# A fused attention and FFN kernel: second batch's attention values in FFN banks, two-bank first FFN blocks, packed sums, more filler matmuls

## The chip, the cores and the metric

One core of one Trainium2 chip. The metric is device time in microseconds (us) of one execution. Where several executions were taken, the median is given. Ratios are the mean time of one kernel's runs over that of the other's of the same rounds, so they are not quite the ratio of the medians that are quoted.

Engines: PE is TensorE, DVE is VectorE, ACT is ScalarE, POOL is GpSimd, SP is SyncE. `L358` in a profile line is line 358 of the kernel; the lines used here have the same numbers in both kernels.

## The reference

```python
# q, k, v: (8, 8, 1024, 64)   E, F: (64, 1024)   w_in: (512, 2048)   w_out: (2048, 512)
k_proj = einsum('ks,bhsd->bhkd', E, k)
v_proj = einsum('ks,bhsd->bhkd', F, v)
scores = q @ k_proj.T / sqrt(64)                  # per batch and head: 1024 x 64
attn   = softmax(scores)
x      = (attn @ v_proj), heads put side by side  # (8192, 512)
out    = (max(x @ w_in, 0) ** 2) @ w_out          # (8192, 512)
```

## The kernel before

Each batch has 1024 tokens, taken as two chunks of 512. For a chunk, FFN does 16 first-layer blocks (4 matmuls of 128x512 each) and then the second layer, in groups of 4 matmuls. Each block or group is a step; a batch has 64 steps. The attention of the next batch is woven in: `at(n, stage)` runs a stage behind step n. Batch 0 has no batch ahead of it, so its own second half runs during its own FFN, and batch 1's attention comes late in the same FFN.

```python
aps = tile_pool(name="aps", bufs=2, space=PSUM)   # attention: 2 tiles of 2 banks
fps = tile_pool(name="fps", bufs=4, space=PSUM)   # FFN and the rest: 4 banks, taken in turn
out_pool = tile_pool(name="outp", bufs=4)         # output rows on their way to memory

def sums(self, pr):                    # packed: two head pairs in one PSUM tile
    ps = att_psum()
    for j in range(2):
        for o, par, a, r in VALUE_QUADS:
            c = 32 * (2 * a + j)
            nc.tensor.matmul(ps[c:c + 32, par], lhsT=ones[r, 0:32], rhs=self.e[pr + j][r, par], ...)
    rs = [soft_pool.tile(...) for _ in range(2)]
    nc.scalar.activation(rs[1][:], ps[:], AF.Ln)                    # L294
    nc.scalar.activation(rs[0][:], rs[1][:], AF.Exp, scale=-1.0)    # L295
    nc.scalar.activation(rs[1][:], rs[1][:], AF.Exp, scale=-1.0)    # L296
    for j in range(2):
        for a in range(2):             # each half-filled tile is completed by copies, L300
            nc.vector.tensor_copy(rs[j][lack:lack + 32], rs[j][have:have + 32])

def chunk_sums(self, c, g):            # plain: one head group, no copies
    ps = att_psum()
    self.sums_mm(ps, self.e[g])
    self.rs[g] = self.inverse(ps)      # Ln and one Exp

def values(self, pr, spare=False):     # spare: in two FFN banks, else in an attention tile
    ...                                # matmuls L312, then xT = values * rs on VectorE, L316

def store(self, c, tb, ps):
    o = out_pool.tile([P, DM], F32)
    nc.scalar.copy(o, ps)              # L371
    nc.sync.dma_start(out_rows[...], o)  # L373
```

Filler matmuls on zeros, `warm(n)`, keep TensorE active in the startup, before the first FFN. (`...` marks cuts.)

The softmax here doesn't subtract the row's maximum and nothing guards it: scores larger than these inputs give would overflow.

Of the kernel before, what the change touches and what calls it, by code (L numbers as in the profile page):

```python
# [18 lines left out]
def kernel(  # L19
# [49 lines left out]
    def bank(shape=(P, 512), dtype=F32):  # L69
        return fps.tile(list(shape), dtype, tag="bank", name="ps_bank")  # L70
# [18 lines left out]
    K0, Q0, V0 = (qkv_pool.tile([P, H, NI, D], BF16, name=n) for n in ("K_sb", "Q_sb", "V_sb"))  # L89
# [42 lines left out]
    def projection(name, e_bf):  # L132
        ps = bank([P, NI, KP], BF16)
        view = e_bf[:].rearrange("k (p i) -> k i p", i=NI)
        for i in range(NI):
            nc.tensor.transpose(ps[:, i, :], view[:, i, :], ident[0:KP, 0:KP])
        t = const_pool.tile([P, NI, KP], BF16, name=name)
        nc.vector.tensor_copy(t[:], ps[:])
        return t

    def warm(n):

        ps = bank()
        for _ in range(n):
            nc.tensor.matmul(ps[:], lhsT=zeros[:, 0:P], rhs=zeros[:], start=True, stop=True)
# [5 lines left out]
    class Attention:  # L151
# [29 lines left out]
        def project(self):  # L181
            ps = bank()
            for i in range(NI):
                f, l = i == 0, i == NI - 1
                nc.tensor.matmul(ps[LO, :], lhsT=ET[:, i, :], rhs=self.K[:, :, i, :], start=f, stop=l)  # L185
                nc.tensor.matmul(ps[HI, :], lhsT=FT[:, i, :], rhs=self.V[:, :, i, :], start=f, stop=l)
            for g in range(2):
# [11 lines left out]
        def project_v(self, g):  # L199

            ps = bank()
            for i in range(NI):
                for o in (LO, HI):
                    nc.tensor.matmul(
                        ps[o, 0:C // 2], lhsT=FT[:, i, :], rhs=V0[:, half[g], i, :],
                        start=(i == 0), stop=(i == NI - 1),
# [138 lines left out]
    class Ffn:  # L345
# [29 lines left out]
        def steps(self):  # L375
            for c in range(2):
                self.hsq[c] = hsq_pool.tile([P, NFB, TCH], BF16, name="hsq")
                first = self.cold and c == 0
                fb0 = 0
                if first:  # L380

                    banks = [bank() for _ in range(4)]
                    for g, fbs in ((0, (0, 1)), (0, (2, 3)), (1, (0, 1)), (1, (2, 3))):
                        for fb in fbs:
                            for cb in (2 * g, 2 * g + 1):
                                self.first_mm(c, fb, cb, banks[fb])
                            if g == 1:
                                self.square(c, fb, banks[fb])
                        yield
                    fb0 = 4  # L390
                for fb in range(fb0, NFB):
                    ps = bank()
                    for cb in range(NCB):
                        self.first_mm(c, fb, cb, ps)
                    self.square(c, fb, ps)
                    yield
                if first:

                    for t0 in range(0, 4, 2):
                        banks = [bank() for _ in range(2)]  # L400
                        for j in range(WP):
                            for t in range(2):
                                for fb in range(j * fn, (j + 1) * fn):
                                    self.second_mm(c, t0 + t, fb, banks[t])
                                if j == WP - 1:
                                    self.store(c, t0 + t, banks[t])
                                yield
                else:
                    last = self.b == B - 1 and c == 1
                    for tb in range(4):  # L410
                        if last and tb == 3:

                            for m in (slice(0, DM // 2), slice(DM // 2, DM)):
                                ps = bank()
                                for fb in range(NFB):
                                    self.second_mm(c, tb, fb, ps, m)
                                self.store(c, tb, ps, m)
                            break
                        ps = bank()
                        for j in range(WP):  # L420
                            for fb in range(j * fn, (j + 1) * fn):
                                self.second_mm(c, tb, fb, ps)
                            if j == WP - 1:
                                self.store(c, tb, ps)
                            yield

    with tc.manual_schedule(engines={PE}):
        e_bf = soft_pool.tile([KP, S], BF16, tag="expT", name="e_bf")
        nc.vector.tensor_copy(e_bf[:], e_f32[:])
        warm(8)  # L430
        ET = projection("ET", e_bf)
        warm(3)
        att = Attention(0)
        att.project_k(0)
        att.transpose_q_chunk(0, Q0, 0)
        att.transpose_k((0,))
        warm(1)
        att.chunk_scores(0, 0)
        FT = projection("FT", f_bf)
        att.project_k(1)  # L440
        att.chunk_sums(0, 0)
        att.transpose_q_chunk(0, Q0, 1)
        att.transpose_k((1,))
        warm(2)
        att.chunk_scores(0, 1)
        warm(4)
        att.project_v(0)
        att.chunk_sums(0, 1)
        warm(1)
        att.chunk_values(0, 0)  # L450
        warm(1)
        att.project_v(1)

        coming = None
        for b in range(B):
            plan = {}

            def at(step, fn, *args, **kwargs):
                plan.setdefault(step, []).append(lambda: fn(*args, **kwargs))

            if b == 0:
                at(1, att.chunk_values, 0, 1)
                at(20, att.transpose_q_chunk, 1, Q0, 0)
                at(20, att.transpose_q_chunk, 1, Q0, 1)
                at(22, att.chunk_scores, 1, 0)
                at(22, att.chunk_scores, 1, 1)
                at(25, att.chunk_sums, 1, 0)
                at(25, att.chunk_sums, 1, 1)
                at(29, att.chunk_values, 1, 0)
                at(29, att.chunk_values, 1, 1)  # L470
                nxt = Attention(1)
                nxt.load()
            if b + 1 < B:
                if b + 2 < B:
                    coming = Attention(b + 2)
                    coming.load()
                if b == 0:
                    at(36, nxt.project)
                    at(37, nxt.transpose_q, 0)
                    at(37, nxt.transpose_q, 1)  # L480
                    at(39, nxt.transpose_k)
                    at(41, nxt.scores, 0)
                    at(41, nxt.scores, 1)
                    at(43, nxt.transpose_q, 2)
                    at(43, nxt.transpose_q, 3)
                    at(45, nxt.sums, 0)
                    at(45, nxt.values, 0)
                    at(51, nxt.values, 1, True)
                    at(51, nxt.scores, 2)
                    at(51, nxt.scores, 3)  # L490
                    at(55, nxt.sums, 2)
                    at(55, nxt.values, 2)
                    at(55, nxt.values, 3, True)
                else:
                    at(14, nxt.scores, 0)
                    at(14, nxt.scores, 1)
                    at(18, nxt.sums, 0)
                    at(18, nxt.values, 0, True)
                    at(18, nxt.scores, 2)
                    at(27, nxt.values, 1)  # L500
                    at(27, nxt.scores, 3)
                    at(49, nxt.sums, 2)
                    at(49, nxt.values, 2)
                    at(49, nxt.values, 3, True)
                if b + 2 < B:
                    if b == 0:
                        at(61, coming.project)
                        at(63, coming.transpose_q_dma)
                        at(64, coming.transpose_k)
                    else:  # L510
                        at(27, coming.project)
                        at(30, coming.transpose_q_dma)
                        at(29, coming.transpose_k_dma)
            for step, _ in enumerate(Ffn(att, b == 0).steps(), 1):
                for stage in plan.pop(step, []):
                    stage()
            assert not plan, plan
            att, nxt = nxt, coming
# [30 lines left out]
```

## Time and profile before

| | before |
|---|---|
| time | 513.74 us, median of 3 (513.23 to 514.64); 513.52 of 6 |
| span in the profile | 511.5 us |
| TensorE busy | 98% |
| start of batch 1's FFN | 91.94 us |
| from there to the end | 419.6 us |

The page of the profile, kernel before: the span, one engine line of its first part (busy us, share of the span, instructions) and the granted clock and DMA rows in 40 slices.

```profile
span 511.5 us, 6926 instructions
...
PE 502.2 (98%) x2756; PEld 223.6 (44%) x2756; DVE 213.6 (42%) x433; ACT 273.7 (54%) x412; POOL 32.1 (6%) x44
...
PEclk9999999999999999999999999999999999999999
DMA  9999999899996199104931060100102011010102
```

TensorE has hardly any idle time to win, and what there is lies in the first slices, where the DMA row is full as well. One slice is 12.8 us, so the full part reaches past 60 us.

The waits of TensorE over the whole span, kernel before (who waited for whom: us in total, times, longest):

```profile
PE ps_bank L194 <- DMA K_sb<-in_k_dram: 1.2, 2, 0.6
...
PE ps_bank L241 <- DMA Q_sb<-in_q_dram: 0.8, 1, 0.8
PE ps_att L256 <- DVE xT L316: 0.8, 1, 0.8
PE ps_bank L231 <- DMA Q_sb<-in_q_dram: 0.7, 2, 0.4
...
PE ps_bank L358 <- DVE xT L341: 0.2, 1, 0.2
```

The timeline of TensorE, kernel before (start, length, engine, line, operation, in the brackets the idle time before it and what ended it). The length is modelled for pipelined matmuls; the start of the next group is the safer end of a group.

```profile
20.88 1.04 PE L358 MATMUL ps_bank<-xT,w_in_114 128*128 128x512 bf16 x4
...
22.19 1.04 PE L358 MATMUL ps_bank<-xT,w_in_116 128*128 128x512 bf16 x4
23.12 0.38 PE L358 MATMUL ps_bank<-xT,w_in_114 128*128 128x512 bf16 x1
23.72 0.81 PE L358 MATMUL ps_bank<-xT,w_in_114 128*128 128x512 bf16 x3 [0.22 <-DVE xT L341]
...
39.64 1.07 PE L231 MATMUL ps_bank<-ident,Q_sb 128*128 128x128 bf16 x16 [0.44 <-DMA Q_sb<-in_q_dram]
...
58.30 1.04 PE L358 MATMUL ps_bank<-xT,w_in_118 128*128 128x512 bf16 x4
60.16 1.07 PE L241 MATMUL ps_bank<-ident,Q_sb 128*128 128x128 bf16 x16 [0.82 <-DMA Q_sb<-in_q_dram]
...
76.05 0.39 PE L256 MATMUL ps_att<-qT,kT 64*64 64x512 bf16 x4
77.19 0.41 PE L256 MATMUL ps_att<-qT,kT 64*64 64x512 bf16 x4 [0.76 <-DVE xT L316]
```

A 128x512 matmul starts 0.216 us after the one before it in an undisturbed stretch (16 in 3.45 us). The four at 58.30 should be done at 59.16, but the next group starts at 60.16: a hole of 1.00 us. In the same way there is a hole of 0.60 us before 39.64. The four small scores matmuls at 76.05 take about 0.22 us by their starts (the like-sized group of L312 just before them took 0.24), so the hole before 77.19 is about 0.92 us. After 92 us the table of waits has nothing. So the change has about 2.5 us to win after 25 us, and something before that.

The windows view, kernel before (stretch and its length; busy us and instructions of PE, PEld, DVE, ACT, POOL; then the granted clock, the DMA share and GB/s):

```profile
8.50:11.90 3.40, 2.29 (x30) 1.49 (x31) 1.59 (x4) 1.39 (x2) 1.49 (x2) 1.00 1.28 202
11.90:15.30 3.40, 3.40 (x22) 2.17 (x23) 0.75 (x2) 0.95 (x1) 1.48 (x2) 0.50 1.28 206
```

For 3.4 us the clock was at half after a stretch in which TensorE was busy for 2.3 of 3.4 us. The length agrees with the Trainium skill ("TensorE: Matmul & The Clock Gate", Part 1), which gives a free-running window of 3413 ns whose activity sets the clock to half or full.

### The profile page before, as it was taken

The page shows a single profiled execution, that of the slowest core. Times are in us where ns is not written, and L with a number is a line of the kernel's source. Part 1 is how long each engine was busy: PE and PEld are TensorE (multiplying, and loading weights), DVE is VectorE, ACT ScalarE, POOL GpSimd, SP SyncE. Part 2 cuts the span into 40 slices and gives each one's busy share as a digit, 9 for nine tenths or more (in the row PEclk, how much of TensorE's full clock was granted, in tenths as well). Part 3 has the DMA queues.
Part 4 walks back from the last instruction along what each step waited for, and adds up shares of the span by engine and source line. Part 5 has one row for each costly group of instructions (what it writes and reads, how often), then busy time and mean ns, then how long its engine had stood idle before and what let it go on. Part 6 is the DMA issues. An engine that isn't in the chain of part 4 may idle for free.

```text
span 511.5 us, 6926 instructions
## 1 busy us (share of the span) xinstructions
PE 502.2 (98%) x2756; PEld 223.6 (44%) x2756; DVE 213.6 (42%) x433; ACT 273.7 (54%) x412; POOL 32.1 (6%) x44
## 2 busy tenths in 40 slices
PE   7999999999999999999999999999999999999997
PEld 3444444444444444444444444444444444444444
DVE  2441666544444445345352354434443443522130
ACT  2565475673637556375654837366472755544351
POOL 7320100121000020001000000000000000000000
PEclk9999999999999999999999999999999999999999
DMA  9999999899996199104931060100102011010102
GB/s 161 204 205 222 227 207 201 129 217 205 195 214 124 43 183 210 71 0 91 201 88 45 1 161 16 60 24 32 63 1 81 2 41 42 25 59 21 62 1 82
DMA packets 67840, 53.92 MB, mean 105 GB/s; under 512 B 29152, under 2 KB 59616, under 8 KB 67808
## 3 DMA queue, kind: packets, MB, share of 16 engines
q0 software_dynamic: 30880, 29.49, 36.4%
q1 hardware_dynamic: 36928, 23.99, 17.8%
q8 instruction: 21, 0.34, 0.3%
q14 instruction: 11, 0.09, 0.1%
HBM read 59.24 MB, written 16.78 MB: 149 GB/s over the span
## 4 chain that ended last, share of the span: by engine, by line
PE 87%; DMA 11%; issue 1%; DVE 0%; POOL 0%; ACT 0%; POOLq 0%; ACTq 0%
PE ps_bank L364 40%; PE ps_bank L358 40%; DMA Q_sb<-in_q_dram 6%; DMA w_in_122<-in_moe_w_in_dram 3%; PE ps_bank L185 2%; DMA K_sb<-in_k_dram 2%; PE ps_att L256 1%; PE ps_att L290 1%; PE ps_att L312 1%; PE ps_bank L312 1%; PE ps_bank L241 0%; DVE rs L300 0%; ACT rs L296 0%; POOL K_sb L76 0%; DVE xT L316 0%
## 5 line engine op out<-in xcount | busy, mean ns | idle before, releaser
L355 DVE TENSOR_TENSOR hsq<-h_relu 128x512 bf16<-128x512 bf16 x256 | 108.7, 425 | 192.5 <-ACT h_relu L354 191.8
L354 ACT ACTIVATE h_relu<-ps_bank 128x512 bf16<-128x512 f32 x256 | 151.8, 599 | 69.5 <-PE ps_bank L358 69.4
L364 PEld LDWEIGHTS <-hsq 128*128 128x128 bf16 x1040 | 99.7, 98 | 122.9 <-issue 9.3
L371 ACT COPY o_sb<-ps_bank 128x512 f32<-128x512 f32 (+1 forms) x65 | 37.5, 579 | 111.1 <-PE ps_bank L364 105.0
L364 PE MATMUL ps_bank<-w_out_128,hsq 128*128 128x512 bf16 (+1 forms) x260 | 65.8, 376 | 0.0
L364 PE MATMUL ps_bank<-w_out_124,hsq 128*128 128x512 bf16 (+1 forms) x260 | 65.7, 376 | 0.0
L364 PE MATMUL ps_bank<-w_out_131,hsq 128*128 128x512 bf16 (+1 forms) x260 | 65.6, 376 | 0.0
L364 PE MATMUL ps_bank<-w_out_126,hsq 128*128 128x512 bf16 (+1 forms) x260 | 65.6, 376 | 0.0
L358 PE MATMUL ps_bank<-xT,w_in_122 128*128 128x512 bf16 x256 | 59.1, 379 | 0.0
L358 PE MATMUL ps_bank<-xT,w_in_118 128*128 128x512 bf16 x256 | 58.2, 379 | 0.0
L358 PE MATMUL ps_bank<-xT,w_in_120 128*128 128x512 bf16 x256 | 58.2, 379 | 0.0
L300 DVE COPY rs<-rs 32x1024 f32<-32x1024 f32 x56 | 38.6, 690 | 42.3 <-ACT rs L295 41.5
L270 ACT ACTIVATE expT<-ps_att 128x1024 bf16<-128x1024 f32 x32 | 31.8, 1023 | 25.3 <-PE ps_att L256 25.2
L358 PEld LDWEIGHTS <-w_in_122 128*128 128x128 bf16 x256 | 24.5, 98 | 31.2 <-issue 2.7
L358 PEld LDWEIGHTS <-w_in_120 128*128 128x128 bf16 x256 | 24.9, 98 | 30.1 <-issue 0.4
L358 PEld LDWEIGHTS <-w_in_118 128*128 128x128 bf16 x256 | 24.9, 98 | 29.9 <-issue 0.4
L358 PE MATMUL ps_bank<-xT,w_in_114 128*128 128x512 bf16 x128 | 30.6, 379 | 0.2 <-DVE xT L341 0.2
L358 PE MATMUL ps_bank<-xT,w_in_116 128*128 128x512 bf16 x128 | 30.4, 379 | 0.0
L316 DVE TENSOR_TENSOR xT<-ps_att,rs 128x512 bf16<-128x512 f32 x28 | 18.1, 686 | 9.2 <-PE ps_att L312 8.9
L294 ACT ACTIVATE rs<-ps_att 128x1024 f32<-128x1024 f32 x14 | 14.3, 1023 | 12.7 <-PE ps_att L290 12.7
L358 PEld LDWEIGHTS <-w_in_114 128*128 128x128 bf16 x128 | 12.4, 98 | 15.3 <-issue 0.9
L358 PEld LDWEIGHTS <-w_in_116 128*128 128x128 bf16 x128 | 12.4, 98 | 15.1 <-issue 0.2
(71 smaller groups left out, 236.6 us busy)
## 6 DMA issues: line engine op xcount, KB each, us to landing
out_dram<-o_sb SPq DMA_DIRECT2D x63, 256.0 KB, 2.0
K_sb<-in_k_dram POOLq DMA_DIRECT2D x7, 1024.0 KB, 22.2
V_sb<-in_v_dram POOLq DMA_DIRECT2D x7, 1024.0 KB, 26.7
Q_sb<-in_q_dram POOLq DMA_DIRECT2D x7, 1024.0 KB, 14.8
K_sb<-in_k_dram POOLq DMA_DIRECT2D x2, 512.0 KB, 7.0
V_sb<-in_v_dram POOLq DMA_DIRECT2D x2, 512.0 KB, 11.1
Q_sb<-in_q_dram POOLq DMA_DIRECT2D x2, 256.0 KB, 7.5
w_in_118<-in_moe_w_in_dram POOLq DMA_DIRECT2D x1, 512.0 KB, 14.9
```

The costliest lines, as they stand in the source:

```text
L185: nc.tensor.matmul(ps[LO, :], lhsT=ET[:, i, :], rhs=self.K[:, :, i, :], start=f, stop=l)
L256: nc.tensor.matmul(ps[o, par], lhsT=self.kT[r, h % 4, h // 4, :], rhs=self.qT[r, h, n, :], start=True, stop=True)
L270: nc.scalar.activation(e[:], ps[:], AF.Exp, scale=SCALE)
L294: nc.scalar.activation(rs[1][:], ps[:], AF.Ln)
L300: nc.vector.tensor_copy(rs[j][lack:lack + 32], rs[j][have:have + 32])
L312: nc.tensor.matmul(ps_x[par][o], lhsT=self.vp[r, 2 * pr + a, :], rhs=e[r, par], start=True, stop=True)
L316: nc.vector.tensor_tensor(out=self.xT[:, pr, :, par], in0=ps_x[par].rearrange("p (c t) -> p c t", c=2), in1=rs[:, par].rearrange("p (c t) ...
L354: nc.scalar.activation(r[:], ps[:], AF.Relu)
L355: nc.vector.tensor_tensor(out=self.hsq[c][:, fb, :], in0=r[:], in1=r[:], op=ALU.mult)
L358: nc.tensor.matmul(ps[:], lhsT=w_in_blk(cb, fb), rhs=self.xT[:, cb, c].rearrange("p a t -> p (a t)"), start=(cb == 0), stop=(cb == NCB - 1),)
L364: nc.tensor.matmul(ps[:, m], lhsT=self.hsq[c][:, fb, tb * P:(tb + 1) * P], rhs=w_out_blk(fb)[:, m], start=(fb == 0), stop=(fb == NFB - 1),)
L371: nc.scalar.copy(o[:, m], ps[:, m])
```

## The change

The intent has three parts: fillers to keep the clock full and first FFN blocks that hold two banks, not four; Q transposes later, so that they do not wait for their load; batch 1's first values in FFN's banks, so that the attention tile is free for the scores. The second half's sums become packed. Cut to its core:

```diff
-                    banks = [bank() for _ in range(4)]
-                    for g, fbs in ((0, (0, 1)), (0, (2, 3)), (1, (0, 1)), (1, (2, 3))):
-                        for fb in fbs:
+                    banks = [bank() for _ in range(2)]
+                    for g in range(2):
+                        for fb in range(2):
 ...
-                    fb0 = 4
+                    fb0 = 2
 ... fillers: 3 -> 4, +1, 1 -> 3, +3, 4 -> 2, one moved: five more in all ...
-                at(20, att.transpose_q_chunk, 1, Q0, 0)      # and the second; scores 22 -> 23
+                at(21, att.transpose_q_chunk, 1, Q0, 0)
-                at(25, att.chunk_sums, 1, 0)
-                at(25, att.chunk_sums, 1, 1)
+                at(26, att.sums, 0)
 ...
-                    at(37, nxt.transpose_q, 0)               # and 1
+                    at(39, nxt.transpose_q, 0)
-                    at(43, nxt.transpose_q, 2)               # and 3
+                    at(44, nxt.transpose_q, 2)
                     at(45, nxt.sums, 0)
-                    at(45, nxt.values, 0)
-                    at(51, nxt.values, 1, True)
-                    at(51, nxt.scores, 2)
+                    at(48, nxt.values, 0, True)
+                    at(48, nxt.scores, 2)
+                    at(51, nxt.values, 1)
                     at(51, nxt.scores, 3)
```

More of the change, by code (lines that the diff above doesn't have):

```diff
@@ L431 @@
         ET = projection("ET", e_bf)
-        warm(3)
+        warm(4)
         att = Attention(0)
         att.project_k(0)
+        warm(1)
         att.transpose_q_chunk(0, Q0, 0)
         att.transpose_k((0,))
-        warm(1)
+        warm(3)
         att.chunk_scores(0, 0)
         FT = projection("FT", f_bf)
+        warm(3)
         att.project_k(1)
@@ L445 @@
         att.chunk_scores(0, 1)
-        warm(4)
+        warm(2)
         att.project_v(0)
+        warm(1)
         att.chunk_sums(0, 1)
-        warm(1)
         att.chunk_values(0, 0)
@@ L462 @@
                 at(1, att.chunk_values, 0, 1)
-                at(20, att.transpose_q_chunk, 1, Q0, 0)
-                at(20, att.transpose_q_chunk, 1, Q0, 1)
-                at(22, att.chunk_scores, 1, 0)
-                at(22, att.chunk_scores, 1, 1)
-                at(25, att.chunk_sums, 1, 0)
-                at(25, att.chunk_sums, 1, 1)
+                at(21, att.transpose_q_chunk, 1, Q0, 0)
+                at(21, att.transpose_q_chunk, 1, Q0, 1)
+                at(23, att.chunk_scores, 1, 0)
+                at(23, att.chunk_scores, 1, 1)
+                at(26, att.sums, 0)
                 at(29, att.chunk_values, 1, 0)
@@ L478 @@
                     at(36, nxt.project)
-                    at(37, nxt.transpose_q, 0)
-                    at(37, nxt.transpose_q, 1)
+                    at(39, nxt.transpose_q, 0)
+                    at(39, nxt.transpose_q, 1)
                     at(39, nxt.transpose_k)
@@ L483 @@
                     at(41, nxt.scores, 1)
-                    at(43, nxt.transpose_q, 2)
-                    at(43, nxt.transpose_q, 3)
+                    at(44, nxt.transpose_q, 2)
+                    at(44, nxt.transpose_q, 3)
                     at(45, nxt.sums, 0)
-                    at(45, nxt.values, 0)
-                    at(51, nxt.values, 1, True)
-                    at(51, nxt.scores, 2)
+                    at(48, nxt.values, 0, True)
+                    at(48, nxt.scores, 2)
+                    at(51, nxt.values, 1)
                     at(51, nxt.scores, 3)
```

## The prediction

> **What bounds the kernel now.** TensorE. The page gives PE 98% of a 511.5 us span, and later batches repeat every 60.4 us in the chain of waits with no PE wait in the waits table. So only the first 92 us can change. Comparing starts of successive PE groups in the timeline with 0.216 us per 128x512 matmul, about 10 us there is not useful matmul time, most of it before 25 us. After 25 us only three holes matter: 0.60 us before the second-half Q transposes (39.64), 1.00 us before batch 1's Q transposes (60.16, "DMA Q_sb"), and 0.92 us before one scores group (77.19, "DVE xT"). The chain of waits follows DMA up to 60.16: queues move about 205 GB/s without a break, so loads land at fixed times whatever PE does.
>
> **Startup fillers.** Windows show the clock at 0.50 from about 11.9 to 15.3 us; there eight K-projection matmuls take 1.81 us instead of 0.87. That is one 3.4 us window, as the Trainium skill says ("TensorE: Matmul & The Clock Gate", Part 1: idle window halves the clock). Net five more fillers cost 1.1 us of matmul time but sit mostly in holes (0.39 us at 10.2, 0.59 at 11.85); I give 70% that the clock then stays full. PE gets about 1.3 us ahead before FFN, but V halves land near 15.9 and 18.4 and w_in near 19.7 and 22.
>
> **First FFN blocks over two banks.** This removes useful work: before, w_in_116 matmuls filled 22.19 to 23.12 while VectorE evicted xT. Now PE waits for that eviction (about 1.2 us). Estimated net lead after these blocks: 0.4 us.
>
> **Sums of the second half.** Moving the Q transposes one step later hides the 0.6 us hole; lead about 0.8 us. One packed sums group (0.34 us for 8) replaces two plain ones (0.56), and ScalarE does three 1.0 us passes, not four. But VectorE gets four new 0.69 us rs copies behind the last passes. Estimate: sums at 45.7, Ln and two Exp to 49.3, copies to 51.0, four xT products (0.62 each) to 53.5, while PE wants the last xT block at 52.5. A new wait of about 1 us at the start of the second FFN chunk eats the lead: about 0 left.
>
> **Batch 1.** Q transposes two steps (1.73 us) later: the 1.00 us hole goes. Values in FFN banks with scores a step group earlier should free the attention bank, so the 0.92 us wait for xT goes. But the first second-layer matmul now needs the bank of the relu which queues behind a 1.06 us Exp: a new wait of about 0.4 us. Net 0.3 to 0.5.
>
> **Sum.** 0.0 + 1.0 + 0.3 gives about 1.3 us saved, 0.25%; nothing later changes. Prediction 512.5 us, 80% range 511.2 to 513.7. Faster by over 2%: 0.01; within 2%: 0.98; slower by over 2%: 0.01.
>
> **What would show it.** Right: clock 1.0 through 11.9 to 15.3; a PE wait for xT (L341) near 21 to 22.5 and again near 52; four rs copies (L300) near 48 to 51; no PE wait for Q_sb at 60; no PE wait of 0.8 us for xT (L316), instead a short one for a relu near 74; batch period still 60.4 us. Wrong: clock still halved; no xT wait near 52 (then up to 2.3 us saved); Q_sb landing later than 60.1 us.
>
> **What would make it wrong.** The clock window may fall differently in each run; the rs copies may take longer while another engine shares the memory port; the scores two steps after the transposes may wait for qT or kT.

## The result

| | before | after |
|---|---|---|
| median of 6 | 513.52 us (513.23 to 514.64) | 512.41 us (512.14 to 512.76) |
| ratio | | 0.9976, 95% interval 0.9963 to 0.9988 |
| span in the profile | 511.5 us | 510.6 us |
| start of batch 1's FFN | 91.94 us | 91.03 us |
| from there to the end | 419.6 us | 419.6 us |

The time fell by 1.1 us, and the whole saving in the profiles (0.9 us) is there when batch 1's FFN starts. All outputs are right.

The page of the profile, kernel after:

```profile
span 510.6 us, 6940 instructions
...
PE 501.5 (98%) x2761; PEld 223.0 (44%) x2761; DVE 216.9 (42%) x437; ACT 272.8 (53%) x411; POOL 32.3 (6%) x44
```

The windows view, kernel after, for the stretch whose clock was at half before:

```profile
11.90:15.30 3.40, 2.88 (x34) 1.78 (x34) 1.64 (x4) 1.60 (x2) 1.48 (x2) 1.00 1.29 205
```

The waits of TensorE, kernel after:

```profile
PE ps_bank L358 <- DVE xT L341: 1.8, 5, 0.9
...
PE ps_bank L358 <- DMA w_in_114<-in_moe_w_in_dram: 0.6, 1, 0.6
PE ps_bank L194 <- DMA K_sb<-in_k_dram: 0.4, 1, 0.4
PE ps_bank L204 <- DMA V_sb<-in_v_dram: 0.3, 1, 0.3
```

The three waits named above are gone. In their place stands one for xT, five times, and waits for loads in the startup. The timeline of PE, DVE and ACT, kernel after:

```profile
20.36 1.04 PE L358 MATMUL ps_bank<-xT,w_in_114 128*128 128x512 bf16 x4 [0.63 <-DMA w_in_114<-in_moe_w_in_dram]
...
22.60 0.38 PE L358 MATMUL ps_bank<-xT,w_in_114 128*128 128x512 bf16 x1 [0.87 <-DVE xT L341]
...
49.11 2.80 DVE L300 COPY rs<-rs 32x1024 f32<-32x1024 f32 x4 [6.93 <-ACT rs L295]
51.94 2.48 DVE L341 TENSOR_TENSOR xT<-ps_att,rs 128x512 bf16<-128x512 f32 x4
52.69 0.38 PE L358 MATMUL ps_bank<-xT,w_in_114 128*128 128x512 bf16 x1
53.28 0.38 PE L358 MATMUL ps_bank<-xT,w_in_114 128*128 128x512 bf16 x1 [0.22 <-DVE xT L341]
53.88 0.38 PE L358 MATMUL ps_bank<-xT,w_in_114 128*128 128x512 bf16 x1 [0.22 <-DVE xT L341]
54.48 1.24 PE L358 MATMUL ps_bank<-xT,w_in_114 128*128 128x512 bf16 x5 [0.22 <-DVE xT L341]
...
61.83 1.06 PE L241 MATMUL ps_bank<-ident,Q_sb 128*128 128x128 bf16 x16
...
70.37 1.02 ACT L294 ACTIVATE rs<-ps_att 128x1024 f32<-128x1024 f32 x1
71.28 0.60 ACT L354 ACTIVATE h_relu<-ps_bank 128x512 bf16<-128x512 f32 x1
...
72.70 0.61 ACT L354 ACTIVATE h_relu<-ps_bank 128x512 bf16<-128x512 f32 x1
73.36 1.04 PE L364 MATMUL ps_bank<-w_out_124,hsq 128*128 128x512 bf16 x4
...
76.30 0.39 PE L256 MATMUL ps_att<-qT,kT 64*64 64x512 bf16 x4
76.62 1.04 PE L364 MATMUL ps_bank<-w_out_131,hsq 128*128 128x512 bf16 x4
```

The brackets show only 0.22 us of idle before each matmul at 53.28, 53.88 and 54.48, because a matmul's modelled length is 0.38. By the starts, each came 0.60 us after the one before it, not 0.216: three times 0.38, or 1.14 us, paced by the xT products of 0.62 us each.

Lining up the two timelines at the same work shows where TensorE gained and lost. In the column "after minus before" the work that the change moved across the point is taken out (one step of four matmuls is 0.86 us).

| point | before | after | after minus before | what happened since the last point |
|---|---|---|---|---|
| first second-layer step | 35.59 | 35.93 | +0.34 | startup |
| second-half Q transposes (one step later) | 39.64 | 40.25 | -0.25 | hole of 0.60 gone |
| second FFN chunk | 52.90 | 52.69 | -0.21 | packed sums 0.22 shorter; a wait of 0.27 for a w_out piece |
| its third block | 54.63 | 55.55 | +0.92 | new wait for xT, 1.14 |
| batch 1's Q transposes (two steps later) | 60.16 | 61.83 | -0.06 | hole of 1.00 gone |
| batch 1's FFN | 91.94 | 91.03 | -0.91 | hole of 0.92 gone, no new wait |

### The profile page after: what moved, and what is told of

It is laid out like the page before. It is cut to its first block, busy times and chain, and to the rows that moved or that the text cites. A ratio compares the mean times of both kernels' runs of the same rounds, so it can differ in the third digit from the quotient of the medians.

```text
span 510.6 us, 6940 instructions
## 1 busy us (share of the span) xinstructions
PE 501.5 (98%) x2761; PEld 223.0 (44%) x2761; DVE 216.9 (42%) x437; ACT 272.8 (53%) x411; POOL 32.3 (6%) x44
## 4 chain that ended last, share of the span: by engine, by line
PE 90%; DMA 7%; POOL 1%; DVE 1%; issue 1%; ACT 0%; POOLq 0%; ACTq 0%
PE ps_bank L364 42%; PE ps_bank L358 41%; DMA w_out_131<-in_moe_w_out_dram 4%; DMA w_in_116<-in_moe_w_in_dram 3%; PE ps_bank L185 2%; PE ps_att L256 1%; PE ps_att L290 1%; PE ps_att L312 1%; PE ps_bank L312 1%; DVE rs L300 0%; DVE xT L341 0%; PE ps_bank L241 0%; POOL K_sb L76 0%; POOL V_sb L76 0%; POOL Q_sb L76 0%
## 5 line engine op out<-in xcount | busy, mean ns | idle before, releaser
L300 DVE COPY rs<-rs 32x1024 f32<-32x1024 f32 x60 | 41.7, 695 | 47.4 <-ACT rs L295 46.5
L358 PE MATMUL ps_bank<-xT,w_in_122 128*128 128x512 bf16 x256 | 59.1, 379 | 0.0
L358 PE MATMUL ps_bank<-xT,w_in_120 128*128 128x512 bf16 x256 | 58.0, 379 | 0.0
L358 PE MATMUL ps_bank<-xT,w_in_118 128*128 128x512 bf16 x256 | 58.0, 379 | 0.0
L358 PEld LDWEIGHTS <-w_in_120 128*128 128x128 bf16 x256 | 25.0, 98 | 30.4 <-issue 0.4
L358 PEld LDWEIGHTS <-w_in_118 128*128 128x128 bf16 x256 | 24.9, 98 | 30.2 <-issue 0.4
L358 PEld LDWEIGHTS <-w_in_122 128*128 128x128 bf16 x256 | 24.4, 98 | 31.0 <-issue 2.7
L358 PE MATMUL ps_bank<-xT,w_in_114 128*128 128x512 bf16 x128 | 31.0, 379 | 2.4 <-DVE xT L341 1.8
L358 PE MATMUL ps_bank<-xT,w_in_116 128*128 128x512 bf16 x128 | 30.2, 379 | 0.0
L294 ACT ACTIVATE rs<-ps_att 128x1024 f32<-128x1024 f32 x15 | 15.4, 1024 | 13.4 <-PE ps_att L290 13.4
L358 PEld LDWEIGHTS <-w_in_114 128*128 128x128 bf16 x128 | 12.4, 98 | 17.9 <-issue 3.0
L358 PEld LDWEIGHTS <-w_in_116 128*128 128x128 bf16 x128 | 12.5, 98 | 15.1
```

Source lines behind the costliest of these rows:

```text
L358: nc.tensor.matmul(ps[:], lhsT=w_in_blk(cb, fb), rhs=self.xT[:, cb, c].rearrange("p a t -> p (a t)"), start=(cb == 0), stop=(cb == NCB - 1),)
```

## The experiments

Two theories come from this table. Theory A: the loads pace TensorE until about 42 us, so the startup part gives nothing; the packed sums give back what the later Q transposes win; the moved values are the saving. Rival B: the clock kept full in the startup is the saving. Other rivals are named with the runs. Each experiment was timed in five rounds (e6 and e11 have six times), with the kernel before in the same rounds.

A caution on the profiles: the first load of K lands about 6 us after its issue in most of them, but after 7.3 and 7.8 us in two (e3 and e8). Those two profiled executions were the slowest of their kernel's five, 1.0 and 0.7 us above the next. Medians are compared for this reason, and the timelines only from a common point on.

| run | median us | before in the same rounds | ratio, 95% interval | batch 1's FFN at | from there to the end |
|---|---|---|---|---|---|
| e1 startup part only | 513.54 | 513.39 | 0.9998 (0.9985 to 1.0011) | 92.30 | 419.5 |
| e2 later part only | 512.48 | 513.39 | 0.9982 (0.9965 to 0.9999) | 90.98 | 420.1 |
| e3 change, plain sums | 512.26 | 513.39 | 0.9979 (0.9963 to 0.9994) | 91.84 | 420.0 |
| e4 change, values back | 513.24 | 513.39 | 0.9996 (0.9979 to 1.0013) | 91.96 | 419.5 |
| e5 change again | 512.86 | 513.49 | 0.9985 (0.9972 to 0.9998) | 90.99 | 419.5 |
| e6 change, plain sums | 512.37 | 513.49 | 0.9986 (0.9966 to 1.0006) | 90.02 | 420.4 |
| e7 change, Q at step 37 | 512.76 | 513.49 | 0.9980 (0.9968 to 0.9992) | 91.18 | 419.5 |
| e8 plain sums, Q at step 37 | 512.90 | 513.49 | 0.9988 (0.9976 to 1.0000) | 92.54 | 419.5 |
| e9 values moved only | 513.34 | 513.60 | 0.9989 (0.9976 to 1.0001) | 91.40 | 420.6 |
| e10 plain sums, 8 output buffers | 511.51 | 513.60 | 0.9960 (0.9948 to 0.9972) | 90.14 | 419.5 |
| e11 change, 8 output buffers | 512.26 | 513.60 | 0.9981 (0.9966 to 0.9996) | 91.27 | 419.4 |
| e12 as e10, four first banks | 511.48 | 513.60 | 0.9960 (0.9948 to 0.9972) | 90.02 | 419.5 |

The intervals reach 0.6 to 1.0 us to each side. Smaller differences between two runs are not shown by the times alone; where one is explained below, the explanation rests on the profiles, one execution of each kernel.

### e1: the startup part alone

```diff
-        warm(3)
+        warm(4)                 # and the other fillers of the change, in the kernel before
 ...
-                    banks = [bank() for _ in range(4)]
+                    banks = [bank() for _ in range(2)]      # with the block order of the change
```

> The kernel before with only the startup part of the change (the fillers and the first FFN blocks over two banks). Theory A (loads pace TensorE until about 42 us, the saving comes from the later steps): within 0.4 us of before, with the clock full from 12 to 15 us but batch 1 starting within 0.4 us of 91.9. Rival B (the saving is the clock kept full in the startup): 0.9 to 1.3 us faster than before, like the whole change.

Measured: no change (513.54 against 513.39). The clock was full from 9.1 us on (by the lengths of the matmuls; the clock column of the windows view shows 1.00 earlier too), batch 1's FFN started at 92.30 instead of 91.94, and the waits for Q_sb (1.0 us, before 0.8) and for xT at the attention tile (0.8 us, as before) were still there. Rival B falls. Another look supports this: in e7's profile the first twelve fillers and the first K projection ran at half clock until about 9.7 us, where the whole change had the full clock from about 4 us, and yet it reached the first second-layer step at 35.82, where the whole change was at 35.93.

### e2: the later part alone

```diff
-        warm(4)
+        warm(3)                 # and the other fillers of before, in the whole change
 ...
-                    banks = [bank() for _ in range(2)]
+                    banks = [bank() for _ in range(4)]      # with the block order of before
```

> The kernel before with only the later-step part of the change (shifted Q transposes, packed sums, values in FFN banks), startup as before. Theory A: 0.9 to 1.5 us faster than before, no wait for Q_sb at 60 us, no wait for xT at 77 us, a wait for xT of about 1 us near 53. Rival B: within 0.3 us of before.

Measured: 0.91 us faster by the medians, just inside what theory A expected, and 90.98 us at batch 1's FFN although the clock was at half from 12.1 to 15.5 us. The later part is the whole change as far as batch 1's start goes. But the rest took 420.1 us, not 419.5, with a new wait of 0.4 us "L358 <- ACT o_sb". That wait was not in theory A yet; e6 and e10 take it up.

### e3 and e6: plain sums in place of packed ones

```diff
-                at(26, att.sums, 0)
+                at(25, att.chunk_sums, 1, 0)
+                at(25, att.chunk_sums, 1, 1)
```

> The whole change, but the second half's sums plain again (two groups after step 25 instead of one packed group after step 26). Theory A says the packed sums with their four copies cost a 1.1 us wait at the second FFN chunk: this run is 0.7 to 1.0 us faster than the whole change, about 2.0 us faster than before, unless the Q_sb landing at 60.1 us takes some of it. Rival C (the wait near 53 us is not caused by the copies but by TensorE being early, so it only moves): within 0.3 us of the whole change.

> Plain sums in the rest of the change, repeated because the profile of the first look fell in an execution whose first load landed 1.5 us late. Theory A: batch 1 starts near 90.1 us, 0.9 us earlier than in the whole change, and the run is 0.6 to 1.0 us faster than it. Rival E (the first loads of an execution land by chance and the steps before 42 us hide nothing, so plain sums only move the wait): within 0.3 us of the whole change, with a wait for a load in place of the wait for xT.

Measured: in both profiles no wait for xT near 53 us is left, and in e6 batch 1's FFN starts at 90.02, the 0.97 us earlier than in e5 that theory A expected. But the time hardly followed. e3 was 1.1 us faster than before, no better than the whole change, so its expectation was missed; e6 was 0.49 us faster than e5 by the medians, less than the 0.6 expected. Rival C falls: the wait near 53 us is that of the packed sums, and without them it does not turn up anywhere before batch 1. Rival E is right that something further on takes the time back, though it is no load. The profile of e6 shows where the lead went. Timeline of PE, ACT and SP, e6 (the tile names lack their numbers in the experiments):

```profile
141.94 12.34 SPq L373 DMA_DIRECT2D out_dram<-o_sb  x5
...
150.39 0.59 ACT L371 COPY o_sb<-ps_bank 128x512 f32<-128x512 f32 x1 [6.07 <-DMA out_dram<-o_sb]
150.44 2.75 PE L358 MATMUL ps_bank<-xT,w_in 128*128 128x512 bf16 x12
153.32 0.59 ACT L371 COPY o_sb<-ps_bank 128x512 f32<-128x512 f32 x1 [2.35 <-DMA out_dram<-o_sb]
153.96 2.32 PE L358 MATMUL ps_bank<-xT,w_in 128*128 128x512 bf16 x10 [0.77 <-ACT o_sb L371]
```

The first of the five output stores, issued at 141.94, landed after 11.3 us (by the chain of waits, which runs through it). Until then its output buffer was taken, the copy at 153.32 waited for the buffer, and TensorE at 153.96 for the PSUM bank that this copy empties: 0.77 us. In the kernel before and in the whole change the last of these copies waited 0.35 and 0.52 us for its buffer, and no PE wait followed. They were at the edge of this floor. How early TensorE comes does not decide it alone: e3 and e9, which started batch 1's FFN at 91.84 and 91.40, had a wait of this kind (0.3 and 0.8 us), and e5 and e7, at 90.99 and 91.18, had none. How late the store lands in that execution counts as well.

### e4: batch 1's values and third scores as before

```diff
-                    at(48, nxt.values, 0, True)
-                    at(48, nxt.scores, 2)
-                    at(51, nxt.values, 1)
+                    at(45, nxt.values, 0)
+                    at(51, nxt.values, 1, True)
+                    at(51, nxt.scores, 2)
```

> The whole change, but batch 1's first values and third scores at the steps and in the banks of before. Theory A: the wait for xT near 77 us is back with 0.8 to 0.9 us, so the run is 0.7 to 0.9 us slower than the whole change and 0.1 to 0.4 us faster than before. Rival D (the wait is hidden by the other moves): within 0.3 us of the whole change.

Measured: the wait is back, and nearly the whole saving is lost (513.24 against 513.39; batch 1's FFN at 91.96). The waits of TensorE, e4:

```profile
PE ps_bank L358 <- DVE xT L341: 1.7, 5, 0.9
...
PE ps_att L256 <- DVE xT L316: 0.8, 1, 0.8
```

Rival D falls: this hole is not hidden by the other moves.

### e5, e7 and e8: does the later Q transpose matter?

e5 is the whole change again; e7 and e8 put the transposes back.

```diff
-                    at(39, nxt.transpose_q, 0)      # and 1
+                    at(37, nxt.transpose_q, 0)
 (e7: in the whole change; e8: in the change with plain sums)
```

> The whole change once more, to be compared on one chip with the next three. All theories: 0.9 to 1.3 us faster than before. Batch 1 starts at about 91.0 us in the trace.

> The whole change with batch 1's first Q transposes back at step 37. Theory A: the wait for xT near 53 us has already made TensorE so late that it reaches the transposes at about 60.1 us, when Q_sb lands at 60.4, so only 0.2 to 0.5 us are lost against the whole change. If waits simply add up (rival F), 1.0 us is lost and the run equals the kernel before.

> Plain sums and the Q transposes back at step 37. Theory A: TensorE reaches the transposes at about 59.2 us and waits 1.0 to 1.2 us for Q_sb, so what plain sums saved is lost again: within 0.3 us of the run before it in this list (packed sums, step 37). Rival F: 0.9 us faster than that run.

Measured: e5 was 0.63 us faster than before, less than the 0.9 expected and than in its first rounds; its five times spread from 512.21 to 513.65. e7 was 0.10 us faster than e5 by the medians, and started batch 1's FFN 0.19 us later, with a Q_sb wait of 0.2 us; theory A had 0.2 to 0.5 us lost, which the times do not show. So undoing the move costs next to nothing in the whole change, and rival F (waits add up) falls: TensorE comes late enough because of the xT wait. With plain sums it has no such wait, and then it waits for Q_sb. The waits of TensorE, e8:

```profile
PE ps_bank L194 <- DMA K_sb<-in_k_dram: 2.2, 1, 2.2
...
PE ps_bank L241 <- DMA Q_sb<-in_q_dram: 0.8, 1, 0.8
```

e8 and e7 are 0.14 us apart, as theory A said; the wait of 0.8 us is under its 1.0 to 1.2. The profile of e8 is one with late first loads (the 2.2 us), so its position at batch 1's FFN is not compared.

### e9: the moved values alone

```diff
-                    at(45, nxt.values, 0)           # in the kernel before, nothing else
-                    at(51, nxt.values, 1, True)
-                    at(51, nxt.scores, 2)
+                    at(48, nxt.values, 0, True)
+                    at(48, nxt.scores, 2)
+                    at(51, nxt.values, 1)
```

> The kernel before with three moved lines only: batch 1's first values go to FFN's banks after step 48, its third scores go there with them, its second values use the attention bank. Theory A: this alone removes the 0.8 us wait for xT near 77 us, so batch 1 starts near 91.0 us and the run is 0.8 to 1.1 us faster than before, as much as the whole change. If the startup, the Q moves or the packed sums carry a real part of the saving (rival G), it is at least 0.4 us slower than the whole change.

Measured: a miss in the time, only 0.26 us faster by the medians, with the five times from 512.51 to 513.97. In the trace the part does what it should: from batch 1's Q transposes to its FFN 30.94 us, where the kernel before took 31.78; it starts batch 1's FFN at 91.40 and not near 91.0 because the Q transposes, which wait for Q_sb, started 0.30 us later than before. The profiled execution then took 420.6 us for the rest: its store at 143.23 landed after 11.5 us, and TensorE waited 0.8 us for the copy, as in e6. So the time that the moved values save can be handed back at 154 us even with less lead than the whole change has, when the store is slow. By the time alone rival G's expectation is met: the median is 0.5 to 0.9 us above those of the whole change. It is put down to this wait, which is shown for one execution only. Against rival G stand the traces and e4, where taking the moved values out of the change loses nearly all of the saving.

### e10 and e11: eight output buffers

```diff
-    out_pool = ctx.enter_context(tc.tile_pool(name="outp", bufs=4))
+    out_pool = ctx.enter_context(tc.tile_pool(name="outp", bufs=8))
 (e10: in the change with plain sums; e11: in the whole change)
```

> Plain sums in the rest of the change, and eight output buffers in place of four. Theory A: the lead that plain sums give is handed back at 154 us, where an output store of 11 us keeps an output buffer, the copy waits for the buffer and TensorE for the bank (0.8 us). With eight buffers that wait is gone: the span is 419.6 us after the start of batch 1, the run 1.9 to 2.3 us faster than before. Rival H (the wait at 154 us is one execution's chance): no different from plain sums, about 1.1 us faster than before.

> Control: the whole change with eight output buffers. Theory A: TensorE comes to 154 us about when the buffer is free, so this is 0.0 to 0.3 us faster than the whole change, 1.0 to 1.4 us faster than before.

Measured: e10 was 2.09 us faster than before and e11 1.34, both as expected; rival H falls. Timeline of ACT and PE, e10:

```profile
143.87 0.59 ACT L371 COPY o_sb<-ps_bank 128x512 f32<-128x512 f32 x1 [2.87 <-PE ps_bank L364]
...
147.32 0.59 ACT L371 COPY o_sb<-ps_bank 128x512 f32<-128x512 f32 x1 [2.87 <-PE ps_bank L364]
150.57 5.78 PE L358 MATMUL ps_bank<-xT,w_in 128*128 128x512 bf16 x26
150.77 0.59 ACT L371 COPY o_sb<-ps_bank 128x512 f32<-128x512 f32 x1 [2.87 <-PE ps_bank L364]
```

Every copy now waits only for its matmuls, and first-layer matmuls run on. With the buffers, plain sums are worth 0.75 us more than packed ones by the medians (e10 against e11, same rounds; 1.13 us at batch 1's FFN in the profiles), where without them e3 and e6 showed little. Two of e11's six executions took 513.97 us; no profile shows why.

### e12: the first FFN blocks over four banks again

```diff
-                    banks = [bank() for _ in range(2)]      # in e10; the new fillers stay
+                    banks = [bank() for _ in range(4)]      # with the block order of before
```

> Fillers of the change, but the first FFN blocks over four banks as before, plain sums and eight output buffers. Theory A: the 1.1 us wait for xT at 22 us goes, but the last w_out piece lands at 42.2 us whatever TensorE does, so it equals the run with two banks, plain sums and eight buffers within 0.3 us. If the startup counts after all: 0.7 to 1.0 us faster than that run.

Measured: 0.03 us from e10. The two-bank order costs something early: e12 reached the first second-layer step at 35.28, e10 at 36.00. But the loads take it back. Timeline of TensorE, e12:

```profile
39.66 1.07 PE L231 MATMUL ps_bank<-ident,Q_sb 128*128 128x128 bf16 x16
40.56 1.03 PE L364 MATMUL ps_bank<-w_out,hsq 128*128 128x512 bf16 x4
42.20 1.02 PE L364 MATMUL ps_bank<-w_out,hsq 128*128 128x512 bf16 x4 [0.60 <-DMA w_out<-in_moe_w_out_dram]
```

The last w_out piece is there at 42.2 us, and TensorE waits for it. In e10, which comes later, the two groups of four at that place take 2.06 us instead of 1.73. At the second half's sums the two stand at 45.54 and 45.66.

e10 and e12 beat both kernels.

## Why the prediction was right

The time, 512.41 us, lay 0.1 us from the predicted 512.5. That close a hit was luck in part: the prediction took about 1.3 us off the median of three (513.74), the median of six is 513.52, and the saving was 1.1 us, a sum of terms of which two were off. Point by point:

- **Startup: right that the clock stays full, wrong that it gives a lead.** The step "estimated net lead after these blocks: 0.4 us" failed: the traces show +0.34 us (later), and e1 shows no saving in the time. The term that was off is "about 1.3 us ahead before FFN". TensorE was 1.51 us ahead at the first V projection (16.05 against 17.56), but then it waited 0.28 us for V_sb and 0.63 for w_in_114, and began FFN only 0.52 us ahead (20.36 against 20.88). From there to the first second-layer step the two-bank order took 0.86 us longer, about the 0.9 that the prediction had for it. A larger lead would not have been kept either. What I had not put into the sum is the last w_out piece, which lands between 41.7 us (before) and 42.4 us (e1) in the profiles with normal first loads (e12: TensorE waits 0.6 us for it). In these runs a lead of the startup ends at it: e12 is 0.7 us ahead of e10, which has the two-bank order, at the first second-layer step, and this vanishes there.
- **Second-half Q transposes: right in kind.** The hole went; the lead after them was 0.25 us, not 0.8, since the startup's 0.4 was missing.
- **Packed sums: right.** Predicted a wait of about 1 us at the second FFN chunk; measured 1.14 us in three pieces, behind four copies from 49.11 to 51.91 us (predicted end 51.0). e6 removes it and starts batch 1 0.97 us earlier.
- **Batch 1's Q transposes: right.** The 1.00 us hole went. e7 adds what the prediction did not say: once the packed sums have made TensorE 0.92 us late, it meets Q_sb almost as it lands, and undoing the move costs only 0.19 us at batch 1's FFN. In the whole change the move only makes room for that lateness.
- **Moved values: mechanism right, one term mis-sized.** The step "a new wait of about 0.4 us" for the bank of the queued relu did not come. The relu started at 72.70 and was done at 73.31, and the matmul that needed its bank started at 73.36. I had added up the lengths of ScalarE's operations. Done with the lengths of the trace, from the relu at 69.88 over Ln, relu and Exp, that puts the end of this relu at 73.78, a wait of 0.42 us. But in the trace the next operation starts before the length of the last one is over: the Ln at 70.37 with 1.02 us is followed at 71.28. The Trainium skill says it ("ScalarE: Activation LUTs", "What ACT_TABLE_LOAD costs"): back-to-back activations overlap by about 93 ns; here it is 0.11 us. Where an activation reads the output of the one before there is none: the Ln at 46.97 with 1.02 us is followed by its Exp at 48.02. So the saving was 0.85 us, not 0.3.
- **The sum.** Predicted 0 + 1.0 + 0.3; the trace has +0.92 late, then 0.98 and 0.85 gained, 0.91 in all. The missed startup lead (0.92 us late where about 0 was expected) and the missing relu wait (0.85 where 0.3 was expected) partly cancelled each other. This was luck: the total was closer than its parts.
- **Nothing later changes: right for the profiled execution (419.6 us both), but it holds by a narrow margin.** e2, e3, e6 and e9 show a wait for the output store at 154 to 155 us that a little more lead, or a slower store, brings out.

## What to carry to other kernels

When loads arrive at fixed times, write down for each stage when its load lands: a saving ahead of such a time is kept only as far as that floor allows, and two changes can compensate each other at it, so test parts in pairs and not only one by one. When an expected gain is in the trace at one point and not in the time, compare the length of the rest of the run: here a wait 60 us further on, for one of four output buffers, had taken it. Use the distance between starts, not the sum of lengths, to place queued operations.

What stays open: why the stores near 142 us take so long was not tested: 8.6 us in the median before (2.2 to 12.9) and 9.0 after (8.7 to 9.4), 11.3 and 11.5 for the ones that e6 and e9 waited for (SP issues them right behind a DMA transpose); whether the slow executions of e9 all have the wait that its profile shows; and why the first load of some executions lands 1.5 us later.

## What the Trainium skill lacked or had wrong

- "ScalarE: Activation LUTs": the overlap of back-to-back activations is there, but under the heading on table loads; it is confirmed (0.11 us here, 0.093 there), and here it decided whether a queued relu made TensorE wait. That passage lacks that an activation which reads the output of the one before does not overlap with it: the Exp at 48.02 started 0.03 us after the end of its Ln.
- "TensorE: Matmul & The Clock Gate" says that the window is free-running and that the start of a kernel varies by it. The start does vary: the filler matmuls reached the full clock at about 4 to 5 us in some executions (before, after) and at about 9.1 and 9.7 us in others (e1, e7), by their lengths. It lacks that a full clock can be worth nothing when loads pace the startup: e1 gained nothing with the clock full from 9.1 us on.
- No page that I used gives the landing time of a 256 KB output store that is issued behind DMA transposes: 8.6 us in the median near 142 us in the kernel before and up to 12.9, up to 13.8 in e9, against a median of 2.0 us over the whole of the kernel before.
